# A transformer block on one core: new durations for the order's planner, SyncE issues held back by one planned microsecond, fifteen weight corrections moved from VectorE to ScalarE and GpSimd

## The chip, the core and the metric

The kernel runs on one core of a Trainium2 chip (trn2). The metric is the device time of one execution in microseconds (us), as the median of several runs. One profiled execution lies beside the timed runs; all rows of the profile come from it.

## What is computed

A transformer block over 2048 tokens of width 640: layer norm, sliding-window attention with 32 heads of size 20 and a window of 256 keys, output projection and residual, then layer norm, a GEGLU feed-forward of width 1536, and residual. All inputs and the output are float32.

```python
def _A_ref(x, wqkv, wo):            # B, S, D = 1, 2048, 640
    H = 32; Dh = D // H; W = 256
    qkv = (x @ wqkv).reshape(B, S, 3, H, Dh).transpose(2, 0, 3, 1, 4)
    q, k, v = qkv[0], qkv[1], qkv[2]
    scores = jnp.einsum("bhqd,bhkd->bhqk", q, k) * (Dh ** -0.5)
    mask = (idx[:, None] - idx[None, :] >= 0) & (idx[:, None] - idx[None, :] < W)
    scores = jnp.where(mask[None, None], scores, -1e9)
    p = softmax(scores)
    return einsum("bhqk,bhkd->bhqd", p, v).transpose(0, 2, 1, 3).reshape(B, S, D) @ wo
def _B_ref(x, w_gate, w_up, w_down):
    return (gelu_tanh(x @ w_gate) * (x @ w_up)) @ w_down
h = x + _A_ref(layernorm(x), A_wqkv, A_wo)
out = h + _B_ref(layernorm(h), B_w_gate, B_w_up, B_w_down)
```

## The kernel before

**Numbers.** Float32 factors are split into a high and a low float16 part, and a product is three float16 matmuls (high by high, high by low, low by high). Each weight matrix W is scaled by a power of two `sc` and split by a `Weight` object: its high part `hl[0]` is made by ScalarE (`split`), its low part `hl[1]` = W·sc − high by a task `low`, one per slice of 128 rows. `low` has two forms. Without `spread`, VectorE does it in one `scalar_tensor_tensor`. With `spread`, ScalarE first scales the slice of W in place and GpSimd then subtracts the high part. A matrix is `ready` when all its low slices are made, and only then may the matmuls that read it be ordered.

**Weights.** `load_lane` brings the output projection and the first gate and up matrices (`w3`, and `gu` in the trace) in slices through a ring of three buffers `wsl`, each slice twice: once for the maximum that gives `sc`, once to be split. A ring buffer is free again when `low` is done with it. The later feed-forward matrices come whole through one buffer `wst`, and of each of these two slices already take the `spread` form.

**Stages.** 16 blocks of 128 tokens, in 8 chunks of two for q and k. Normed x blocks (`xh`, `xl`) are turned by DMA transposes; q and k of a chunk are projected (`mm` banks), leave through `qks` to DRAM and come back stacked by head (`qT`, `kT`). For each block and each pair of heads there are two visits to the score banks `ra` and `rb`: a *maxima* unit (scores in one orientation, reduced on VectorE by the operation that the trace calls `CUSTOM_DVE_ANT_0 junk<-ra,band`, one per head), and, once the row maxima have been put into `qT` through `mT`, a *scores* unit (the other orientation, exponentiated by ScalarE into `pt`, cut to the band by GpSimd's affine selects). Four heads then make a *value* unit (`pv`). Then come normalisation, transposes, the output projection with the residual (`ht`), and a store of the block to `h_dram`. The first feed-forward product runs under the end of the attention; after the attention come three plain (chunk, group) products and then nine "quads" groups, whose matmul order is written out.

TensorE works in three modes: full products, row mode (maxima and scores, 64 rows each) and column mode (values, 32 columns each).

**The order.** Nothing in this kernel is ordered by hand before the quads. Each piece of work is a generator ("lane") that yields the engines it needs and the planned time at which its operands are there. At build time a loop advances a planned clock `now` and always steps the first lane in a list of priorities whose `start(now)` holds; the instruction it emits is booked on that engine with a cost from `Engine.cost`. So `cost` sets no time on the chip, only the order of instructions on each engine. On the chip each engine works its own list strictly in order, waiting at semaphores. The planner puts two units of row work (a maxima and a scores unit, as a rule) into one visit to row mode if the second bank is planned to come free within `APART` = 1.0 us (`row_need`). When no score has been made yet and TensorE is planned to be idle, the loop emits a small dummy matmul on `pv`.

A DMA on SyncE's queue is ordered when `need() <= now + 0.1` for its lane: loads of x and of the residual, the stores to `h_dram`, the DMA transposes, the stacking loads of q and k (lane `stack`), weights (`load_lane`).

Of the kernel before, what the change touches and what calls it, by code (L numbers as in the profile page):

```python
# [24 lines left out]
KC = D // P  # L25
# [9 lines left out]
SWITCH = 0.095  # L35
# [18 lines left out]
class Clock:  # L54
# [90 lines left out]
    def warmth(self, cost, rows):  # L145

        k = int(self.t["tensor"] / self.WINDOW)
        if k > self.win:
            u = self.use / self.WINDOW if k == self.win + 1 else 0.0
            self.warm = u > 0.4 if self.warm else u > 0.75  # L150
            self.win, self.use = k, 0.0
        if not self.warm:
            cost *= 2
        self.use += cost * rows / 128
        return cost
# [34 lines left out]
class Engine:  # L190
# [23 lines left out]
    def cost(self, op, out, ins):  # L214
        n = out.free_size()
        if op.startswith("dma_start"):
            size = math.prod(c for _, c in out.ap) * mybir.dt.size(out.dtype)
            if op == "dma_start_transpose":
                return size / 150e3
            wide = mybir.dt.size(out.dtype) == 4 or out.space == DRAM  # L220
            return size / (380e3 if wide else 150e3)
        half = mybir.dt.size(out.dtype) == 2 and ins and mybir.dt.size(ins[0].dtype) == 2
        if self.name == "tensor":
            n = ins[1].free_size()
            if op == "transpose":
                n = ins[0].partition_size()
            passes = 1 if mybir.dt.size(ins[0].dtype) == 2 else 2 if op == "transpose" else 4
            rows, cols = ins[0].partition_size(), out.partition_size()
            mode = "full" if op == "transpose" else "row" if rows <= 64 else "col"
            mode = "full" if mode == "col" and cols > 32 else mode  # L230
            k = self.clock
            switch, k.mode = SWITCH * (k.mode != mode), mode
            at = out.start_partition() + (ins[0].start_partition() // 4 if mode == "row" else 0)
            beside, k.half = mode != "full" and at > k.half and not switch, at
            if beside:
                return 0.004
            return switch + k.warmth(max(n * passes / 2400, 0.027), rows) + 0.0027
        if self.name == "vector":
            m = max([n] + [i.free_size() for i in ins])
            if op == "tensor_copy" and half or op == "tensor_scalar" and m > 320:  # L240
                return (0.065 if half else 0.185) + 0.00053 * m
            return 0.065 + 0.00106 * m + 0.06 * (op == "scalar_tensor_tensor" and len(ins) == 3)
        if self.name == "scalar":
            return 0.00084 * n + (0.05 if op == "copy" or len(ins) == 1 else
                                  0.14 if ins[0].space == PSUM else 0.18)
        if self.name == "gpsimd":
            if op == "memset":
                return 0.06 + 0.0008 * n
            return 0.46 if n == 1 else 0.06 + (0.00105 if op == "affine_select" else 0.00203) * n
        raise NotImplementedError(self.name)  # L250


# [1 line left out]
def block_kernel(ctx: ExitStack, tc: tile.TileContext, x, wqkv, wo, wg, wu, wd, out):  # L254
# [27 lines left out]
    def done(name):  # L282
# [12 lines left out]
    NW, AHEADQ = 3, 6  # L295
    SPREAD = 0
# [5 lines left out]
    FFBACK = dict(split_lane=0.4, scale_lane=0.4, chunk_lane=0.3, token_sums=0.1,  # L302
                  sums_lane=0.2, norm_lane=0.2)
    EARLY = 0.6
    PACE = 1.0
    SWAY = 4

# [12 lines left out]
    def on(eng, *reads, when=None, after=None):  # L320
        f = need(*reads, when=when, eng=eng)
        if after is not None:
            return (eng,), lambda: max(f(), nc.others(after, eng))
        return (eng,), f
# [214 lines left out]
    def products(n, term, ready=None, at_=None):  # L539


        ps = [at_[0]] if at_ else []
        col = at_[1] if at_ else 0

        def start(i):
            if ready and not ready(i) or not ps and opened["mm"] >= banks["mm"]:
                return INF
            t = nc.ready([x for ab in term(i) for x in ab], "tensor")
            return t if ps else max(t, nc.slot(psums["mm"], "mm", banks["mm"]))

        for i in range(n):
            yield ("tensor",), lambda i=i: start(i)
            if not ps:
                ps.append(bank("mm"))
            m = term(i)
            for k, (l, r) in enumerate(m):
                if k:
                    yield pe()
                o = ps[0][:, col:col + r.free_size()]
                nc.tensor.matmul(o, l, r, start=(i == 0 and k == 0),  # L560
                                 stop=(i == n - 1 and k == len(m) - 1))
                pos["dense"] += r.free_size() * 3 // len(m)
        return o
# [19 lines left out]
    wq = wqp.enter_context(tc.tile_pool(name="wq", bufs=1, side="right"))  # L583
    wp = attn.enter_context(tc.tile_pool(name="wp", bufs=1))
# [3 lines left out]
    gu = ffw.tile([P, 4 * KC * 512], F16, name="gu")  # L588
# [3 lines left out]
    gu = gu.rearrange("p (a c f) -> p a c f", c=KC, f=512)  # L592
# [174 lines left out]
    def stack(c, which, d):  # L767
# [10 lines left out]
        for par in range(2):  # L778
            for m, i in enumerate(((0, 0, 1), (0, 1, 0))[which]):
                rows = slice(64 * par + DH * m, 64 * par + DH * m + DH)  # L780
                if c > 1:
                    yield ("sync",), lambda: nc.moved["sync"] - PACE
                nc.sync.dma_start(to[rows], d.rearrange("(a d i) m n -> a m d i n", a=2,
# [652 lines left out]
    def split_lane():  # L1436
        for i, w in [(1, weights[1]), (0, weights[0]), *enumerate(weights)][:2] + list(
                enumerate(weights))[2:]:
            yield on("scalar", when=lambda: w.scaled)
            if i <= NW:  # L1440
                yield from w.split(wq if i < NW else wp, SPREAD)
                continue
            yield on("scalar", when=lambda: W["v"].ready)
            kind, fg = later[i - NW - 1]
            if fg == 0 and kind != "d":
                a = 2 * (kind == "u")
                yield from w.split((gu[:, a], gu[:, a + 1]))
                continue
            k = 1 if fg else 0
            yield on("scalar", when=lambda: ffpools[k])  # L1450
            yield from w.split(ffpools[k], 2)
# [106 lines left out]
    class Lane:  # L1558
# [11 lines left out]
        def start(self, now):  # L1570

            if "tensor" in self.engs:
                return nc.t["tensor"] <= now + AHEAD and self.need() <= max(now, nc.t["tensor"])
            name = self.gen.__name__
            back = self.back
            if name in ("split_lane", "scale_lane"):
                back = PREP if not W["o", 0].ready else FFPREP
            elif name == "x_lane":
                back = EARLY if not B[XF].full else LATE
            elif name == "max_out" and not W["v"].ready:  # L1580
                back = RAMPMAX
            if isinstance(self.engs, Soon):
                back = max(back, OUT)
            if ffpools[1]:
                back = FFBACK.get(name, OUT)
            return (all(nc.t[e] <= now + back for e in self.engs if e != "sync")
                    and self.need() <= now + 0.1)

    load_x(0)
    load_x(1)  # L1590
# [3 lines left out]
    for i, n in enumerate("qkv"):  # L1594
        W[n].load(rooms[n])
        W[n].room(wq)
        if i:
            load_x(i + 1)
    load_x(NR)
    lanes = [x_lane([0], "x"), x_lane([1], "xb"), x_lane([2], "xc"), x_lane([3], "xd"),  # L1600
             x_lane(range(NR, NB), "x"),
             split_lane(), *(scale_lane([i], str(i)) for i in range(NW)),
             scale_lane(range(NW, len(weights)), "0"), load_lane(), ones_lane(), big_lane(),
             first_norm_lane()]
# [6 lines left out]
    now = 0.0  # L1611
# [85 lines left out]
```

## Time and profile before

| | |
|---|---|
| median of 3 runs | 1022.13 us (1021.41 to 1023.31) |
| profiled execution, its own time | 1023.17 us |
| its span, first to last instruction | 1021.3 us |
| TensorE (PE) busy | 999.8 us, 98% |
| VectorE (DVE) busy | 754.8 us, 74% |
| ScalarE (ACT) busy | 437.0 us, 43% |
| GpSimd (POOL) busy | 298.0 us, 29% |
| granted TensorE clock | 1.000 |

Between span and time lie 1.87 us. In the trace every instruction carries line L199, since a helper records all of them, so groups are told apart by their tiles: `w3l<-wsl,sw,w3h` is a low part of the output projection, `gu<-wsl,sw,gu` one of the first gate or up matrix. PEld is the weight load, which overlaps PE. SPq is SyncE's queue of DMA issues. A busy PE is not PE at its peak: matmuls are pipelined, so a matmul's own duration is longer than the distance to the next one.

### The profile page before, as it was taken

What the parts mean: (1) busy time and instruction counts of PE and PEld (TensorE: products, weight loads), DVE (VectorE), ACT (ScalarE), POOL (GpSimd) and SP (SyncE); (2) the same over time, 40 slices, a digit from 0 to 9 for tenths busy, and PEclk for the clock granted to TensorE, in tenths of its full rate; (3) what the DMA queues carried; (4) which work ended last, traced back from release to release, by engine and by line L of the source; (5) the groups of instructions that cost most, each with busy time, mean ns of one, the idle gap of its engine ahead of it and who ended that gap; (6) DMA issues with size and microseconds to landing.
All of it is one profiled execution on the core that took longest, in us unless ns stands there. A gap on an engine that the chain in (4) does not pass through costs nothing.

```text
span 1021.3 us, 30777 instructions
## 1 busy us (share of the span) xinstructions
PE 999.8 (98%) x12921; PEld 695.8 (68%) x12921; DVE 754.8 (74%) x2221; ACT 437.0 (43%) x706; POOL 298.0 (29%) x489
## 2 busy tenths in 40 slices
PE   8999999999999999999999999999999999999998
PEld 7875666676666676776655564567777777777776
DVE  6888998986787787474788788798996975544553
ACT  6514654656555564654558543522222222221220
POOL 7102223443343342342436321255313310000000
PEclk9999999999999999999999999999999999999999
DMA  8657667361551524225033433223553532222211
GB/s 306 137 116 175 184 145 168 81 163 55 91 122 44 114 57 118 42 61 127 3 131 106 92 117 103 78 104 127 161 177 90 161 138 78 78 96 86 78 53 52
DMA packets 105835, 112.67 MB, mean 110 GB/s; under 512 B 38369, under 2 KB 79585, under 8 KB 105697
## 3 DMA queue, kind: packets, MB, share of 16 engines
q1 hardware_dynamic: 93600, 99.97, 35.9%
q10 hardware_dynamic: 12096, 10.75, 3.4%
q8 instruction: 101, 1.65, 0.7%
q14 instruction: 38, 0.30, 0.1%
HBM read 73.73 MB, written 28.84 MB: 100 GB/s over the span
## 4 chain that ended last, share of the span: by engine, by line
PE 82%; DVE 8%; DMA 4%; ACT 2%; issue 2%; SPq 1%; POOL 0%; ACTq 0%; DVEq 0%
PE mm L199 41%; PE pv L199 12%; PE ra L199 11%; PE rb L199 10%; PE tp L199 7%; DVE junk L199 2%; DVE am L199 1%; DVE ht L199 1%; DMA v<-in_wqkv_dram 1%; DMA gu<-in_wqkv_dram 1%; SPq L199 1%; DMA qT<-mT 1%; DVE m L199 1%; ACT pt L199 1%; DMA h_dram<-ht 1%
## 5 line engine op out<-in xcount | busy, mean ns | idle before, releaser
L199 POOL TENSOR_SCALAR_AFFINE_SELECT pt<-pt 128x512 f32<-128x512 f32 x352 | 175.3, 513 | 278.2 <-ACT pt L199 262.6
L199 DVE CUSTOM_DVE_ANT_0 junk<-rb,band 128x320 bf16<-128x320 f32 x230 | 112.5, 489 | 41.3 <-PE rb L199 35.9
L199 DVE CUSTOM_DVE_ANT_0 junk<-ra,band 128x320 bf16<-128x320 f32 x218 | 106.6, 489 | 43.8 <-PE ra L199 38.3
L199 ACT ACTIVATE pt<-ra,esc 128x640 f32<-128x640 f32 (+2 forms) x131 | 99.6, 767 | 66.2 <-PE ra L199 53.3
L199 ACT ACTIVATE pt<-rb,esc 128x640 f32<-128x640 f32 (+2 forms) x125 | 94.9, 766 | 77.2 <-PE rb L199 56.5
L199 PE MATMUL pv<-pt,v 128*21 128x128 f32 x2880 | 104.1, 275 | 1.1 <-ACT oT L199 1.1
L199 PEld LDWEIGHTS <-ah 128*128 128x128 f16 x768 | 75.0, 98 | 29.5 <-issue 2.1
L199 ACT ACTIVATE gel<-gel,ffk 128x512 f32<-128x512 f32 x36 | 26.0, 721 | 138.0 <-DVE gel L199 138.0
L199 PEld LDWEIGHTS pv<-pt,v 128*21 128x21 f32 x2880 | 68.6, 100 | 11.9 <-issue 2.1
L199 PEld LDWEIGHTS <-ws 128*128 128x128 f16 x720 | 70.3, 98 | 8.3
L199 PEld LDWEIGHTS <-kT 62*64 62x64 f16 x2880 | 61.9, 107 | 13.9 <-issue 10.1
L199 PEld LDWEIGHTS <-qT 60*64 60x64 f16 x1280 | 29.8, 104 | 60.3 <-issue 51.3
L199 PEld LDWEIGHTS <-gu 128*128 128x128 f16 x440 | 42.1, 98 | 36.1 <-issue 2.5
L199 DVE SCALAR_TENSOR_TENSOR ht<-mm,ffk,ht 128x320 f32<-128x320 f32 x96 | 52.1, 545 | 10.9 <-PE mm L199 9.0
L199 ACT CAST ah<-gel 128x512 f16<-128x512 f32 x48 | 29.6, 617 | 64.4 <-DVE gel L199 64.2
L199 PE MATMUL mm<-xh,w1h 128*128 128x256 f16 x200 | 54.7, 274 | 1.3 <-DVE qks L199 1.3
L199 PE MATMUL mm<-xl,w1h 128*128 128x256 f16 x200 | 54.7, 273 | 0.0
L199 PE MATMUL mm<-xh,w1l 128*128 128x256 f16 x200 | 54.7, 273 | 0.0
L199 PE MATMUL mm<-w3l,oh 128*128 128x320 f16 x160 | 48.1, 301 | 0.1
L199 PE MATMUL mm<-w2h,xh 128*128 128x320 f16 x160 | 48.1, 300 | 0.0
L199 PE MATMUL mm<-w2h,xl 128*128 128x320 f16 x160 | 48.1, 301 | 0.0
L199 PE MATMUL mm<-w3h,ol 128*128 128x320 f16 x160 | 48.1, 300 | 0.0
(299 smaller groups left out, 2521.3 us busy)
## 6 DMA issues: line engine op xcount, KB each, us to landing
ws<-wsums SPq DMA_DIRECT2D x24, 640.0 KB
qk<-qks ACTq DMA_DIRECT2D x32, 256.0 KB
qT<-qk SPq DMA_DIRECT2D x48, 160.0 KB
kT<-qk SPq DMA_DIRECT2D x48, 160.0 KB
wsums<-ws SPq DMA_DIRECT2D x12, 640.0 KB
ht<-in_x_dram SPq DMA_DIRECT2D x16, 320.0 KB
h_dram<-ht SPq DMA_DIRECT2D x16, 320.0 KB
ht<-h_dram SPq DMA_DIRECT2D x16, 320.0 KB
```

The costliest lines, as they stand in the source:

```text
L199: r = real(*args, **kw)
```

## The change

Three things. The planner's cost function gets other constants. A lane on SyncE alone, other than `stack` and `load_lane`, is ordered only when its operands have been there for `HELD` = 1.0 planned us (before: up to 0.1 us ahead of them). And the low parts of the output projection (5 slices of 128x640) and of the first gate and up matrices (5 slices of 128x512 each) take the `spread` form.

```diff
@@ Engine.cost
-            switch, k.mode = SWITCH * (k.mode != mode), mode
+            switch = (SWITCH + 0.02 * (k.mode == "col")) * (k.mode != mode)
+            k.mode = mode
...
             if beside:
-                return 0.004
+                return 0.0005
...
-            return 0.065 + 0.00106 * m + 0.06 * (op == "scalar_tensor_tensor" and len(ins) == 3)
+            extra = {"reciprocal": 0.16, "tensor_tensor_reduce": 0.11}.get(op, 0.0)
+            extra += 0.06 * (op == "scalar_tensor_tensor" and len(ins) == 3)
+            return 0.065 + 0.00106 * m + extra
         if self.name == "scalar":
-            return 0.00084 * n + (0.05 if op == "copy" or len(ins) == 1 else
+            return 0.03 + 0.00084 * n + (0.05 if op == "copy" or len(ins) == 1 else
                                   0.14 if ins[0].space == PSUM else 0.18)
         if self.name == "gpsimd":
             if op == "memset":
                 return 0.06 + 0.0008 * n
-            return 0.46 if n == 1 else 0.06 + (0.00105 if op == "affine_select" else 0.00203) * n
+            return 0.46 if n == 1 else 0.1 + (0.00105 if op == "affine_select" else 0.00203) * n
@@ block_kernel
+    HELD = 1.0
@@ split_lane
-                yield from w.split(wq if i < NW else wp, SPREAD)
+                yield from w.split(wq if i < NW else wp, SPREAD if i < NW else KC)
...
-                yield from w.split((gu[:, a], gu[:, a + 1]))
+                yield from w.split((gu[:, a], gu[:, a + 1]), KC)
@@ Lane.start
+            late = 0.1 if self.engs != ("sync",) or name in ("stack", "load_lane") else -HELD
             return (all(nc.t[e] <= now + back for e in self.engs if e != "sync")
-                    and self.need() <= now + 0.1)
+                    and self.need() <= now + late)
```

`SPREAD` is 0 and `KC` is 5. `tensor_tensor_reduce` is the maxima operation.

## The prediction

> **What bounds the kernel now.** I read the page first, then the busy time by stretches, then who TensorE waits for in two windows, then single rows of the timeline.
>
> ```profile
> PE 999.8 (98%) x12921; PEld 695.8 (68%) x12921; DVE 754.8 (74%) x2221; ACT 437.0 (43%) x706; POOL 298.0 (29%) x489
> ```
>
> TensorE is the bound over the whole span. Its work is the same after the change: no matmul is added or removed but the dummies. So the time can only move through what stands between matmuls: waits, changes of mode, dummies.
>
> ```profile
> 90.00:200.00 110.00, 104.07 (x1728) 71.20 (x1727) 99.79 (x348) 66.43 (x116) 35.64 (x65) 1.00 0.62 155
> ...
> 677.00:1022.00 345.00, 340.86 (x2543) 248.16 (x2541) 230.26 (x452) 77.84 (x121) 67.09 (x63) 1.00 0.32 104
> ```
>
> The columns are window, length, then busy time of PE, PEld, DVE, ACT, POOL. From 677 on the matmul order is written out and TensorE is busy to within 4 us (345 - 340.86), the end of the program included: I cost the change at nothing there. From 90 to 200, where all fifteen moved low parts lie, VectorE is at 99.79 of 110, close to being a second bound. What TensorE waits for, first from 90 to 200, then from 200 to 677 (total, times, longest, in us):
>
> ```profile
> PE rb L199 <- issue: 1.3, 1, 1.3
> PE rb L199 <- DMA qT<-mT: 1.1, 1, 1.1
> PE rb L199 <- DVE mxs L199: 0.7, 1, 0.7
> PE pv L199 <- ACT oT L199: 0.7, 2, 0.4
> PE rb L199 <- ACT pt L199: 0.6, 1, 0.6
> PE tp L199 <- DVE ht L199: 0.5, 1, 0.5
> PE mm L199 <- DVE qks L199: 0.5, 1, 0.5
> PE ra L199 <- ACT pt L199: 0.2, 1, 0.2
> ```
>
> ```profile
> PE tp L199 <- DVE m L199: 1.4, 4, 0.8
> PE rb L199 <- issue: 1.1, 1, 1.1
> PE mm L199 <- DVE ht L199: 1.1, 2, 0.7
> PE ra L199 <- DMA kT<-qk: 0.8, 1, 0.8
> PE tp L199 <- DVE am L199: 0.7, 1, 0.7
> PE tp L199 <- DVE ol L199: 0.6, 1, 0.6
> PE tp L199 <- ACT oT L199: 0.5, 1, 0.5
> PE tp L199 <- DVE ht L199: 0.4, 1, 0.4
> PE pv L199 <- ACT oT L199: 0.4, 1, 0.4
> PE mm L199 <- ACT gel L199: 0.3, 1, 0.3
> ```
>
> They sum to 5.6 and 7.3 us, 12.9 in all. The two "issue" rows (2.4) name no engine, so no order of the others removes them; 10.5 us are within reach. Of these VectorE causes 5.9 (0.7 + 0.5 + 0.5 + 1.4 + 1.1 + 0.7 + 0.6 + 0.4), ScalarE and DMA 4.6. So the kernel is already near its bound and the change is worth at most about 1% of it.
>
> **The new durations.** Whether they are nearer to the chip can be read off the timeline, by distances from start to start:
>
> ```profile
> 239.73 0.33 PE L199 MATMUL ra<-kT,qT 60*64 60x256 f16 x8
> 239.89 0.31 PE L199 MATMUL rb<-qT,kT 62*64 62x128 f16 x12
> 240.13 0.85 PE L199 MATMUL pv<-pt,v 128*21 128x128 f32 x24
> 240.92 0.28 PE L199 MATMUL mm<-xh,w1l 128*128 128x256 f16 x1
> 241.04 0.27 PE L199 MATMUL mm<-xh,w1h 128*128 128x256 f16 x1
> 241.15 0.27 PE L199 MATMUL mm<-xl,w1h 128*128 128x256 f16 x1
> 241.35 0.33 PE L199 MATMUL rb<-kT,qT 60*64 60x256 f16 x8
> ```
>
> ```profile
> 226.00 0.49 DVE L199 CUSTOM_DVE_ANT_0 junk<-ra,band 128x320 bf16<-128x320 f32 x1 [0.67 <-PE ra L199]
> 226.42 0.08 DVE L199 DVE_READ_ACCUMULATOR2_ANT mxs<- 128x1 f32 x1
> 226.54 0.49 DVE L199 CUSTOM_DVE_ANT_0 junk<-ra,band 128x320 bf16<-128x320 f32 x1
> ```
>
> TensorE took 0.16 for a maxima unit, 0.24 for a scores unit with the change to column mode, 0.79 for a value unit with the change back: 1.19 us. By the code the old costs book 0.163 + 0.273 + 0.779 = 1.215, the new ones 0.145 + 0.241 + 0.768 = 1.154. The old were 2% long, the new are 3% short: no gain in itself. VectorE took 0.54 per maxima operation; the old cost is 0.065 + 0.00106 x 320 = 0.404, the new 0.514. This is the correction that matters: the old order was laid out for a VectorE a quarter faster at its most frequent operation, beside a TensorE slightly slower than the real one, so on the chip VectorE falls behind the plan and TensorE meets its results late. With the new costs both are a few per cent short, and their ratio is about right. I take half of VectorE's 5.9 us as gone, 3.0 us. The waits on ScalarE and DMA (4.6) are dealt anew, with the same sum: ScalarE's and GpSimd's constants move by only 0.03 and 0.04 per instruction. Bounds: all 10.5 gone; or as much again added, +10, since a new order makes new coincidences.
>
> **The low parts.** Prices: what leaves VectorE, what comes to GpSimd and to ScalarE (least, median and longest ns; the last three from the later weights, which take that form already):
>
> ```profile
> L199 DVE SCALAR_TENSOR_TENSOR w3l<-wsl,sw,w3h x5: 876/879/1293, 98.9 to 107.8; 128x640 f16<-128x640 f32 x5
> ```
>
> ```profile
> L199 DVE SCALAR_TENSOR_TENSOR gu<-wsl,sw,gu x10: 731/746/1026, 144.2 to 197.1; 128x512 f16<-128x512 f32 x10
> ```
>
> ```profile
> L199 POOL TENSOR_TENSOR w10l<-wst,w10h x2: 1396/1396/1397, 540.2 to 542.4; 128x640 f16<-128x640 f32 x2
> ```
>
> ```profile
> L199 POOL TENSOR_TENSOR w5l<-wst,w5h x2: 1156/1158/1159, 588.5 to 589.9; 128x512 f16<-128x512 f32 x2
> ```
>
> ```profile
> L199 ACT ACTIVATE wst<-wst,sw x14: 721/722/830, 539.3 to 679.1; 128x512 f32<-128x512 f32 x8, 128x640 f32<-128x640 f32 x6
> ```
>
> VectorE loses 5 x 0.879 + 10 x 0.746 = 11.9 us of its 99.79. ScalarE gains 5 x 0.83 + 10 x 0.72 = 11.4 on its 66.43, GpSimd 5 x 1.396 + 10 x 1.158 = 18.6 on its 35.64: 71% and 49% of 110, so neither becomes a bound. What VectorE's relief is worth at TensorE is bounded by the three waits on it in that window, 1.7 us, half of which is counted above; I take another 0.8. Each part is now finished about 0.83 + 1.40 later than its high part instead of 0.88, so a ring buffer comes free some 1.3 us later and the output projection's weights are ready perhaps 3 us later; its first matmul has projections of q, k and v to stand in for it, so 0, and 3 if these run out.
>
> Against this stands one row:
>
> ```profile
> 542.46 1.40 DVE L199 TENSOR_SCALAR m<-mxs 128x32 f16<-128x32 f32 x1
> ```
>
> A VectorE instruction on 32 columns took 1.40 us while GpSimd's `w10l` subtraction of 1.396 us (second of its two, 542.4) ran, and it is the longest of TensorE's waits on `m` above, 0.8 us. So such a subtraction can hold a short VectorE instruction to its own end. [...] From the rows: fifteen subtractions cover 18.6 of 110 us, 17%; some four blocks put out two such `m` instructions each there, so one or two are hit, at 0.8 us: I take +0.8. Bounds: 0, and 15 x 0.8 = +12 if each hits.
>
> **The held issues.** SyncE works in order, and most of its waiting is on the store's data:
>
> ```profile
> SPq L199 <- DVE ht L199: 219.1, 29, 40.8
> ```
>
> Behind a store stand the next loads, turns and stacking loads; ordering the store 1 us later lets what is planned in that microsecond go ahead. But TensorE's list names a stacked load only once (0.8) and no load or turn of x at all, so little is waiting behind. In return the first feed-forward norm, which overwrites `ht`, waits for the store:
>
> ```profile
> 233.50 0.61 DVE L199 TENSOR_SCALAR ht<-ht,lmvh,lyh 128x640 f32<-128x640 f32 x1 [1.72 <-DMA h_dram<-ht]
> ```
>
> Four blocks do this, and TensorE's waits on `ht` at `tp` (0.5 and 0.4) are what reaches it. I take 0; bounds -0.8 and +4 x 1.0. Turns and loads of x, ordered 1 us later each, cost nothing while the next chunk is a block ahead.
>
> **The sum.** -3.0 - 0.8 + 0.8 + 0 = -3.0 us. The profiled execution took 1023.17 (span 1021.3 and 1.87 around it), which gives 1020.2; the median of the runs shown lies 1.04 lower, so 1022.13 - 3.0 = 1019.1 us, 0.3% faster. A difference of about 0.2% (2 us) is what a measurement of this kernel can tell from none.
>
> **The rivals.**
>
> *Single visits (slower).* The plan pairs two units in a visit if the second bank comes free within 1.0 us. Booking 0.11 more for each of the two operations of a maxima unit frees its bank 0.22 later in the plan. A visit with one unit pays the entry once more (241.15 to 241.35 is 0.20, where such a product followed by another takes 0.11) and, at the planner's 0.095, the way out: 0.19 us. Against: visits lie 1.62 apart (239.73, 241.35), a bank needs 2 x 0.514 and some 0.2 of latency, 1.2, so the pairs hold with 0.4 to spare. They break where VectorE has something else in hand, which is 90 to 200. It decides if over 25 pairs break: 25 x 0.19 = 4.8, against the gain of 3.0, is 1024; 40 make 1027.
>
> *GpSimd in the way (slower).* Instead of one hit, eight to twelve, at `m` and in front of the affine selects that the value units wait for: +6 to +10 in place of 0.8, so 1024 to 1028; it decides from six hits.
>
> *Dealt anew, nothing won (same).* The waits named on VectorE vanish and others of the same size come: 1022.
>
> *All waits gone (faster still).* 10.5 us: 1011.6. Against: DMA and ScalarE waits have no better duration in the new plan.
>
> **How the numbers follow.** Forecast (gain of 2.1 to 7, 1015 to 1020): 0.42. Larger gain: 0.10. Same: 0.17. Single visits: 0.18. GpSimd in the way: 0.13. So faster 0.52, same 0.17, slower 0.31. The likeliest case's own range is 1015 to 1020; to leave out no more than 2 in 10 the range goes from 1011 (all waits gone) to 1027 (40 broken pairs).
>
> **What would show it.** Right: TensorE's waits on VectorE between 90 and 677 fall from 5.9 to about 3; VectorE's busy time from 90 to 200 falls by some 10; the stretch from the first quads group to the end keeps its length. Wrong: more matmul groups on `ra` and `rb` entered singly; `m` instructions of 1.2 to 1.4 us beside `w3l` or `gu` on GpSimd with TensorE waiting behind them; a first maxima or first score that comes later than now, which I have left at no change.

## The result and the profile after

| | before | after |
|---|---|---|
| median, same chip | 1021.77 us (1020.80 to 1023.31, 4 runs) | 1045.72 us (1044.12 to 1046.28, 4 runs) |
| profiled execution, its own time (span) | 1023.17 us (1021.3) | 1046.20 us (1044.5) |
| mean granted TensorE clock | 1.000 | 0.988 |

The ratio is 1.0233 [1.0215, 1.0251]: 2.3% slower, where 0.3% faster was forecast, and the time lies outside the range of 1011 to 1027. The profile's page after, busy times and the granted clock in 40 slices:

```profile
PE 1020.9 (98%) x13189; PEld 720.1 (69%) x13189; DVE 755.0 (72%) x2206; ACT 449.3 (43%) x721; POOL 315.7 (30%) x504
...
PEclk9999899999999999998899999999999999999999
```

TensorE is still the bound, and now it has 268 matmuls more (13189 against 12921) and slices in which its granted clock is below the full one. No other engine became a bound: VectorE's busy time is what it was. The groups of the dummy matmuls (least, median and longest ns, first and last start), before and after:

```profile
L199 PE MATMUL pv<-ident x324: 218/219/312, 2.5 to 74.3; 128*128 128x128 f16 x162
```

```profile
L199 PE MATMUL pv<-ident x592: 219/219/314, 2.5 to 108.8; 128*128 128x128 f16 x198
```

All 268 are dummies, and they go on 34.5 us longer (74.3 to 108.8). They are ordered while no score has been made, so the first score comes late. The timeline of TensorE after, at that place:

```profile
99.76 0.33 PE L199 MATMUL rb<-kT,qT 60*64 60x320 f16 x4
100.02 3.69 PE L199 MATMUL pv<-ident 128*128 128x128 f16 x63
103.64 0.24 PE L199 MATMUL tp<-ident,m 128*64 128x128 f16 x1
...
104.66 4.36 PE L199 MATMUL pv<-ident 128*128 128x128 f16 x75
108.95 0.24 PE L199 MATMUL ra<-qT,kT 62*64 62x128 f16 x1
111.12 0.30 PE L199 MATMUL ra<-qT,kT 62*64 62x128 f16 x7 [1.93 <-DMA qT<-mT]
```

The first score (`ra<-qT,kT`) comes at 108.95, after ten stretches of dummies from 90.55 on, between which stand only seven maxima units and two transposes of `m`. The last 75 dummies fill 4.29 us (104.66 to 108.95), 0.057 each, so 268 are 15.3 us. The score waits for the row maxima `m`, and these come late in VectorE's order: 80 maxima operations stand ahead of the first of them, 64 before (counted over both traces). The group of the first `m` instruction of each block, before and after:

```profile
L199 DVE TENSOR_SCALAR m<-mxs x16: 130/316/1398, 81.2 to 542.5; 128x32 f16<-128x32 f32 x16
```

```profile
L199 DVE TENSOR_SCALAR m<-mxs x16: 170/178/455, 101.1 to 576.3; 128x32 f16<-128x32 f32 x16
```

The first `m` is at 101.1 instead of 81.2. The second loss is the clock. Stretches of after, with the columns of the prediction's windows and the granted clock behind the five busy times:

```profile
112.20:119.00 6.80, 6.40 (x66) 3.56 (x69) 4.25 (x17) 4.70 (x10) 2.63 (x5) 0.50 0.51 106
...
125.90:129.30 3.40, 3.40 (x33) 2.03 (x32) 2.36 (x7) 3.31 (x7) 1.81 (x2) 0.50 0.76 122
484.30:491.10 6.80, 5.91 (x105) 4.21 (x105) 4.19 (x17) 3.32 (x5) 2.84 (x6) 0.50 0.49 94
515.00:521.80 6.80, 6.02 (x84) 4.24 (x83) 4.45 (x18) 3.70 (x5) 2.85 (x6) 0.50 0.94 329
```

TensorE works 21.7 us at half clock (6.40 + 3.40 + 5.91 + 6.02). If nothing there takes more than twice as long, my estimate from products of 128x256 (0.11 from start to start at 125.55, 0.21 at 128.01, where the clock is 0.50), that costs half of it at most, 10.9; in the profiled execution of before there was none ahead of the last microsecond. The other three timed runs of after had mean clocks of 0.991 to 0.995 and took 1044.12 to 1046.28 us, so this part varies from run to run and the time hardly does. Who TensorE waits for after, from 90 to 200 and then from 200 to 677:

```profile
PE rb L199 <- DVE mxs L199: 2.9, 1, 2.9
PE ra L199 <- DMA qT<-mT: 1.9, 1, 1.9
PE ra L199 <- ACT pt L199: 0.8, 1, 0.8
PE rb L199 <- ACT pt L199: 0.2, 1, 0.2
```

```profile
PE rb L199 <- ACT pt L199: 2.4, 3, 0.9
PE ra L199 <- ACT pt L199: 1.7, 3, 0.9
PE pv L199 <- POOL pt L199: 0.7, 3, 0.3
```

With the three rows of 0.2 to 0.3 that are not shown they are 11.4 us against 12.9 before. But the work ahead of the quads, which ended at 670.9 before, goes on to 693.0 after, and behind 677 TensorE has two more waits there, the second in the first quads group:

```profile
PE mm L199 <- DVE ht L199: 1.4, 1, 1.4
PE tp L199 <- DVE ws L199: 1.9, 1, 1.9
```

Over the whole trace its waits are 19.2 us, 17.3 before. So 15.3 of dummies, at most 10.9 of half clock and 1.9 of waits come to at most 28.1, against 23.0 measured between the two profiled executions. The 5.1 between are not resolved. Two parts of them can be seen: at half clock not every distance doubles (from a maxima to a scores unit it is 0.14 at 480.53 and 0.22 at 485.66, in rows shown further below), and TensorE changes its mode nineteen times fewer (counted over both traces; in the prediction's rows a visit starts 0.20 after a product, and a next product 0.11 after it). The waits are nearly as long as before, and yet the kernel is 2.3% slower: most of what it lost is time spent on dummies and at half clock, and neither is a wait.

### The profile page after: what moved, and what is told of

The parts are those of the page before. It is cut to its first block, busy times and chain, and to the rows that moved or that the text cites. A ratio compares the mean times of both kernels' runs of the same rounds, so it can differ in the third digit from the quotient of the medians.

```text
span 1044.5 us, 31321 instructions
## 1 busy us (share of the span) xinstructions
PE 1020.9 (98%) x13189; PEld 720.1 (69%) x13189; DVE 755.0 (72%) x2206; ACT 449.3 (43%) x721; POOL 315.7 (30%) x504
## 3 DMA queue, kind: packets, MB, share of 16 engines
q1 hardware_dynamic: 93600, 99.97, 34.5%
## 4 chain that ended last, share of the span: by engine, by line
PE 87%; DVE 6%; DMA 3%; ACT 2%; issue 1%; SPq 1%; POOL 0%; ACTq 0%; POOLq 0%; DVEq 0%
PE mm L199 43%; PE pv L199 14%; PE ra L199 12%; PE rb L199 10%; PE tp L199 7%; DVE ts L199 1%; SPq L199 1%; ACT pt L199 1%; DMA qk<-qks 1%; DMA kT<-qk 1%; DMA qT<-mT 1%; DMA wst<-in_wu_dram 0%; DVE ht L199 0%; DVE am L199 0%; DVE junk L199 0%
## 5 line engine op out<-in xcount | busy, mean ns | idle before, releaser
L199 DVE CUSTOM_DVE_ANT_0 junk<-ra,band 128x320 bf16<-128x320 f32 x226 | 110.7, 490 | 57.2 <-PE ra L199 52.2
L199 DVE CUSTOM_DVE_ANT_0 junk<-rb,band 128x320 bf16<-128x320 f32 x222 | 108.8, 490 | 52.9 <-PE rb L199 48.3
L199 ACT ACTIVATE pt<-rb,esc 128x640 f32<-128x640 f32 (+2 forms) x128 | 98.9, 777 | 84.1 <-PE rb L199 73.1
L199 ACT ACTIVATE pt<-ra,esc 128x640 f32<-128x640 f32 (+2 forms) x128 | 95.8, 757 | 86.1 <-PE ra L199 80.7
L199 PE MATMUL pv<-pt,v 128*21 128x128 f32 x2880 | 107.1, 279 | 0.8 <-POOL pt L199 0.7
L199 PEld LDWEIGHTS <-kT 62*64 62x64 f16 x2880 | 65.6, 108 | 14.2 <-issue 10.4
L199 DVE SCALAR_TENSOR_TENSOR ht<-mm,ffk,ht 128x320 f32<-128x320 f32 x96 | 52.0, 544 | 15.3 <-PE mm L199 13.4
L199 POOL TENSOR_TENSOR gelt<-gelt 128x256 f32<-128x256 f32 x18 | 15.4, 854 | 112.1 <-ACT gelt L199 112.0
L199 PE MATMUL mm<-xl,w0h 128*128 128x256 f16 x175 | 48.9, 280 | 0.0
L199 PE MATMUL mm<-xh,w0h 128*128 128x256 f16 x175 | 48.9, 279 | 0.0
L199 PE MATMUL mm<-xh,w0l 128*128 128x256 f16 x175 | 48.9, 279 | 0.0
```

Source lines behind the costliest of these rows:

```text
L199: r = real(*args, **kw)
```

## The experiments

With each set of kernels, before was run on the same chip (medians 1021.8 to 1022.9). A ratio is to that before.

**Which part of the change does it.** First the change without the 0.11 of the maxima operation, and that 0.11 alone in the kernel before:

```diff
e1: the changed kernel, with
-            extra = {"reciprocal": 0.16, "tensor_tensor_reduce": 0.11}.get(op, 0.0)
+            extra = {"reciprocal": 0.16}.get(op, 0.0)
e2: the kernel before, with
+            extra = {"tensor_tensor_reduce": 0.11}.get(op, 0.0)
```

> The changed kernel without one number: the 0.11 that the planner's cost adds to each maxima operation. Held issues, GpSimd's low parts and all other new costs stay. Theory A (that one cost): in the program as written 64 maxima operations stand before the first row-maximum instruction m, as in the kernel before, instead of 80, and 335 dummies instead of 592; so the first score comes at about 90 us as before, the clock stays at 1.000 and the time is 1014 to 1024. Theory B (the low parts crowd ScalarE and GpSimd, or delay the output projection) and theory C (the held issues delay SyncE): both are still in, so 1040 to 1046.

> The kernel before with one number changed: the 0.11 on each maxima operation. Theory A: 80 maxima operations before the first m and 578 dummies, first score at about 109 us, time 1036 to 1048. Theories B and C: neither low parts nor held issues are in, so as before, 1020 to 1024.

Measured: e1 1026.30, ratio 1.0037 [1.0019, 1.0054]; e2 1044.02, ratio 1.0199 [1.0161, 1.0236]. One number in the planner's table makes some 20 of the 24 us, and theories B and C are out as the main cause. In e2 the dummies are 578, in e1 335. e1 lies 2 us above theory A's range, which is part of the 4 us taken up below.

Then the parts that are no durations: the old table with the held issues and the low parts, and each of these alone.

```diff
e3: the changed kernel with the cost function of before
e7: the kernel before, with
+            late = 0.1 if self.engs != ("sync",) or name in ("stack", "load_lane") else -HELD
e8: the kernel before, with
+                yield from w.split(wq if i < NW else wp, SPREAD if i < NW else KC)
+                yield from w.split((gu[:, a], gu[:, a + 1]), KC)
```

> The changed kernel with all the old costs: held issues and GpSimd's low parts alone. Theory A: 64 maxima operations before the first m, 324 dummies, time 1016 to 1025, and which side of before it falls tells what the two other parts are worth. Theories B and C: 1040 to 1046.

> The kernel before with the held issues alone. Held issues and low parts together, with the old costs, took 1025.8 against 1022.64. If the held stores are the cause (the first feed-forward norm waits for them: the wait of 2.3 us on ht at 150 us there): 1024 to 1028 here and 1021 to 1023 with the low parts alone. If it is neither by itself but where the transition to the feed-forward falls: both within 1020 to 1026 with no pattern.

> The kernel before with the fifteen low parts on ScalarE and GpSimd alone. Held stores as the cause of the 3 us: 1021 to 1023. Low parts as the cause (the output projection's first product comes at 130 us instead of 115, short VectorE instructions held by GpSimd): 1024 to 1028. My prediction had this part at 0 net.

Measured: e3 1025.80, ratio 1.0029 [1.0011, 1.0046]; e7 1023.16, ratio 1.0010 [0.9995, 1.0026]; e8 1026.58, ratio 1.0040 [1.0023, 1.0057]. The held issues alone cost nothing clear, the low parts alone 4 us.

**Why a longer, seemingly truer booking does harm.** `junk`, the unused output of the maxima operation, has one buffer. The planner's clock already charges for that:

```python
                lat = self.LAT if e != eng else (0.1 if e in ("vector", "gpsimd") else 0.0)
...
        if len(ring) == bufs:
            self.wr[key] = [((0, 128, 0, 1 << 30), "ring", self.quiet(ring[0]))]
```

A tile whose ring of buffers is full counts as written by "ring", which is no engine, so its next writer waits `LAT` = 0.18 after the last use.

Two maxima operations in a row were thus booked 0.404 + 0.18 = 0.584 apart, not 0.404, and the change makes that 0.694. The chip takes 0.534 (median over both traces). Booked at what the chip takes, with one buffer:

```diff
e9: the changed kernel, with
-            extra = {"reciprocal": 0.16, "tensor_tensor_reduce": 0.11}.get(op, 0.0)
+            extra = {"reciprocal": 0.16, "tensor_tensor_reduce": -0.05}.get(op, 0.0)
```

> The whole changed kernel, one junk buffer, with -0.05 instead of +0.11 on the maxima operation, so that with the 0.18 for the buffer the planner books 0.534, the distance that the trace shows for it (0.534 in the median). The two runs with a second junk buffer were not a test of the plan alone: there the chip's distance fell too, from 0.534 to 0.416. A2 (a VectorE booked too slow spoils the order): about as the run without the 0.11, which booked 0.584: 1018 to 1028. If the 0.11's harm had to do with something else that the second buffer happens to mend on the chip: 1034 or more.

Measured: 1027.05, ratio 1.0044 [1.0024, 1.0063]: the 20 us are gone, as in e1. With a second buffer the plan adds no 0.18, and the 0.11 should be harmless:

```diff
e5: the changed kernel, e6: e2 and e11: the kernel before, each with
-            junk = at("junk", [P, 5 * HB], BF16, 1)
+            junk = at("junk", [P, 5 * HB], BF16, 2)
```

> The whole changed kernel, 0.11 included, with two buffers instead of one for junk, the maxima operation's unused output. The run with m put first took back the late first score and no time, so theory A is now this (A2): with one buffer the planner books 0.18 more between two maxima operations, as a wait for the buffer, so before the change it booked 0.404 + 0.18 = 0.584 for what takes 0.54 on the chip, and with the change 0.694: counted twice. A VectorE booked a quarter too slow holds row visits back, projections are used up ahead of the scores, and TensorE has no cover later. With two buffers that wait is gone and the booking is 0.514: by A2 the time falls to 1015 to 1028, the half-clock windows in the attention go, the share of projections done at 400 us falls from 0.83 to 0.78 to 0.80. Rival D: the 0.11 harms by what it does to the order in any case, or the other new costs do: 1036 to 1046.

> The kernel before with the 0.11 and with two buffers for junk, nothing else. A2: the one number that cost 21 us by itself costs nothing once it is not counted twice: 1016 to 1027. Rival D: 1036 to 1046.

> The kernel before with two junk buffers, its old costs, nothing else: booked 0.404, done in 0.416 by the chip. A2: a booking that fits and 0.118 us less for VectorE at each of 512 operations (55 us of its time): 1012 to 1020, faster than before and than the run with 0.11. If VectorE's time is hidden anyway: 1018 to 1024.

Measured: e5 1026.61, ratio 1.0044 [1.0027, 1.0061]; e6 1019.74, ratio 0.9988 [0.9969, 1.0007]; e11 1022.85, ratio 1.0007 [0.9988, 1.0026]. The 0.11 that costs 21 us with one buffer costs nothing with two. But the chip changes too, in the timeline of VectorE in e6:

```profile
299.53 0.49 DVE L199 CUSTOM_DVE_ANT_0 junk<-rb,band 128x320 bf16<-128x320 f32 x1 [0.80 <-PE rb L199]
299.94 0.08 DVE L199 DVE_READ_ACCUMULATOR2_ANT mxs<- 128x1 f32 x1
299.94 0.49 DVE L199 CUSTOM_DVE_ANT_0 junk<-rb,band 128x320 bf16<-128x320 f32 x1
```

The next operation starts 0.41 after the first, not 0.54 as in the prediction's rows: the second buffer takes out 0.12 on the chip (medians 0.416 and 0.534). So e5 and e6 alone don't tell whether the order or the faster VectorE mended it. Two more do. e11 has the faster VectorE and the old booking, and gains nothing, where I had given 1012 to 1020 for a booking that fits the chip: VectorE's time is hidden, as far as one order shows it (e11's order isn't that of before: its first score comes at 74.6). And e10 has the faster VectorE and is booked 0.694:

```diff
e10: the kernel before, with two buffers for junk and
+            extra = {"tensor_tensor_reduce": 0.29}.get(op, 0.0)
```

> The kernel before with two junk buffers and with 0.29 on the maxima operation: the planner books 0.694 per operation, as in the changed kernel, while the chip does it in 0.416. A2: the order alone does the harm, so 1036 to 1060, with 80 maxima operations before the first m, some 600 dummies and half-clock windows, although VectorE is faster than in any kernel with one buffer. If the chip's VectorE time were the cause: at or below the 1019.7 of the run with 0.11 and two buffers.

Measured: 1072.67, ratio 1.0497 [1.0464, 1.0531]. The maxima operation is as fast as in e11 (0.416 in the median), only the order differs, and it costs 50 us, more than I had expected. Two of its windows at half clock, and its longest waits from 200 to 700, on ScalarE:

```profile
465.50:472.30 6.80, 5.83 (x116) 3.47 (x112) 2.55 (x13) 3.37 (x5) 2.55 (x6) 0.50 0.01 2
496.20:506.40 10.20, 9.07 (x152) 5.96 (x152) 4.63 (x20) 4.67 (x7) 4.25 (x9) 0.50 0.37 72
```

```profile
PE ra L199 <- ACT pt L199: 5.3, 8, 0.9
PE rb L199 <- ACT pt L199: 4.1, 6, 0.9
```

It is the picture of after, larger. (It isn't the plan of e2 on a faster chip: the 0.29 books VectorE as busy, where a ring's 0.18 is only a wait, so this plan is harsher.)

**How the order loses it.** With the maxima booked 30% long, the plan holds row visits apart until it expects a bank to be free. Visits in the prediction's rows lie 1.62 apart with three products between (239.73, 241.35). After, at the same place, in TensorE's timeline:

```profile
239.47 0.33 PE L199 MATMUL rb<-kT,qT 60*64 60x320 f16 x4
...
241.74 0.33 PE L199 MATMUL ra<-kT,qT 60*64 60x320 f16 x4
...
243.67 0.33 PE L199 MATMUL ra<-kT,qT 60*64 60x320 f16 x4
```

They are 2.27 and 1.93 apart, with nine and thirteen products between. From 200 to 530, 43 of before's 177 visits have three matmuls of the full mode (products or transposes) ahead of them and one has fewer than two; after, no visit has three or four, 149 of 163 have five or more, and twelve have one or none (counted over both traces). The products are used up early: at 400 us 82% of the projections but only 55% of the scores are made, before 79% and 62%. The other kernels agree: in e2, e4 and e10 the scores made at 400 us are 56, 56 and 53%, in every other kernel of the experiments 60 to 62% (counted over their traces). What comes then, in the timeline of after:

```profile
480.53 0.34 PE L199 MATMUL ra<-kT,qT 60*64 60x128 f16 x8
480.67 0.34 PE L199 MATMUL rb<-qT,kT 62*64 62x128 f16 x12
480.94 0.24 PE L199 MATMUL tp<-ident,m 128*64 128x128 f16 x1
481.90 0.33 PE L199 MATMUL rb<-kT,qT 60*64 60x128 f16 x8 [0.72 <-ACT pt L199]
482.04 0.34 PE L199 MATMUL ra<-qT,kT 62*64 62x128 f16 x12
482.31 0.87 PE L199 MATMUL pv<-pt,v 128*21 128x128 f32 x16
483.46 0.42 PE L199 MATMUL pv<-pt,v 128*21 128x128 f32 x8 [0.29 <-POOL pt L199]
483.81 0.34 PE L199 MATMUL rb<-kT,qT 60*64 60x128 f16 x8
484.28 0.48 PE L199 MATMUL ra<-qT,kT 62*64 62x128 f16 x12
485.66 0.48 PE L199 MATMUL ra<-kT,qT 60*64 60x128 f16 x8 [0.89 <-ACT pt L199]
485.88 0.53 PE L199 MATMUL rb<-qT,kT 62*64 62x128 f16 x12
```

No `mm` stands between the visits, so the exponentials `pt` are waited for, and from 484.28 the same operation takes 0.48 instead of 0.34: half clock, 0.50 from 484.30 on by the row further above.

One more kernel tried the other end, the late first `m`, by putting the lane of the row maxima ahead of the other maxima lanes:

```diff
e4: the changed kernel, with
+        mfirst = [l for l in trans if l.gen.__name__ == "max_rows"]
-        order = (first + early + outs + trans + sides
+        order = (first + mfirst + early + outs + trans + sides
```

> The whole changed kernel, with one more line in the planner: the lane that turns a block's row maxima into m stands ahead of the maxima operations of later blocks (33 maxima operations before the first m instead of 80, 319 dummies instead of 592). Theory A, with the late m as the link: the first score comes before 90 us and most of the 24 us lost come back: 1020 to 1030 if the later half-clock windows (484 to 491 and 515 to 522 us, worth some 7 us) stay, 1012 to 1020 if they go too. If the cost harms in another way than through the late m, or by theories B and C: 1038 or more.

Measured: 1045.94, ratio 1.0219 [1.0184, 1.0255]. The dummies' group and its waits:

```profile
L199 PE MATMUL pv<-ident x319: 219/219/311, 2.5 to 74.0; 128*128 128x128 f16 x160
```

```profile
PE ra L199 <- ACT pt L199: 5.6, 8, 1.1
PE tp L199 <- DVE ws L199: 4.4, 1, 4.4
```

All 268 extra dummies are gone, the first score is at 80.0, and the time is the same: the lost time moves to waits on `pt` and `ws` and to 23.8 us at half clock (five windows, at 0.50 or 0.51). So the late first score, the link that I had given theory A, is not what costs, and the dummies aren't the cause. As I read it, they are one form in which a plan with too little for TensorE to do shows.

**What is left: about 4 us.** The low parts alone cost 4 us (e8), where I had 0. Split:

```diff
e13: the kernel before, with
+                yield from w.split(wq if i < NW else wp, SPREAD if i < NW else KC)
e14: the kernel before, with
+                yield from w.split((gu[:, a], gu[:, a + 1]), KC)
```

> The kernel before, with the low parts of the output projection's five weights alone made by GpSimd. All fifteen low parts by GpSimd, with nothing else changed, had cost 4 us (1026.58), and the first product of the output projection had come at 132.5 instead of 115. Theory L1 (the output projection's weights come ready later, and its products are then missing as cover): nearly all of the cost is here, 1025 to 1028. Theory L2 (each low part on GpSimd holds VectorE or is itself late, so that the cost goes by their number): a third of it, 1023 to 1024. Theory L3 (every other order deals TensorE a few other waits): anything from 1020 to 1029, and the waits that make it up are at places that have nothing to do with these weights.

> The kernel before, with the low parts of the first ten gate and up weights alone made by GpSimd. L1: within 1 us of before, 1021 to 1023. L2: two thirds of the 4 us, 1024 to 1026. L3: anything from 1020 to 1029, by waits that lie elsewhere.

Measured: e13 1018.58, ratio 0.9957 [0.9939, 0.9976], faster, though the output projection's first product comes at 136.1 instead of 115.2; e14 1029.37, ratio 1.0061 [1.0040, 1.0082]. L1 is refuted, and L2 with it (a gain for five parts, a loss for ten). L3's range of 1020 to 1029 misses both as well, by 1.4 and 0.4 us. In e14 one place of loss can be seen, first the wait and then a window:

```profile
PE mm L199 <- ACT ah L199: 2.9, 1, 2.9
```

```profile
595.60:602.40 6.80, 5.72 (x21) 3.00 (x22) 4.88 (x13) 0.39 (x1) 0.00 (x0) 0.50 1.08 209
```

The first down product waits for its activation at 596, some 400 us after the last moved low part (197.1 in the prediction's row), and the half clock behind it costs another 2.9 at most by the same estimate as in after (half of 5.72). The same wait stands in e8 (2.9), and also in e7 (3.1) and e11 (2.7), which move no low part and are not slower than before. So this wait doesn't account for the 4 us by itself, and it lies far from what was edited. That much is left of L3: which waits an order meets. Why five parts gain and ten lose isn't shown.

Then the other new durations, without the 0.11's double count:

```diff
e12: the kernel before, with all new costs but the 0.11, and two buffers for junk
e16: the changed kernel with two buffers for junk and without the low parts by GpSimd
```

> As the run before it (two junk buffers, maxima booked 0.404), with the change's other new costs for TensorE, ScalarE, GpSimd and the reciprocal; no held issues, no low parts. If those costs are worth something: 1 to 5 us below the run with old costs. If they only deal the waits anew: within 4 us of it either way.

> The changed kernel with the second buffer for the maxima's unused output, and without the low parts by GpSimd: all new costs and the held stores stay. The same with the low parts gave 1026.61. If the low parts' 4 us add up whatever the order: 1022 to 1023. If the other new costs (TensorE's switches and waits, the reciprocals, ScalarE's and GpSimd's) are what costs there, as the 1031.42 of all new costs but the 0.11 suggest: 1026 to 1031. L3: anything between.

Measured: e12 1031.42, ratio 1.0077 [1.0050, 1.0104]; e16 1024.37, ratio 1.0021 [0.9997, 1.0045]. e12 lost 8.6 us against e11, more than the 4 either way that I had allowed; in e16 the same costs, with the 0.11 and the held issues, lose nothing clear. So these costs have no price of their own either.

**A version that beats both, and what it is worth.** The best of e6 with the held issues, then the same without its 0.11, and with the low parts that had won in e13:

```diff
e15: the kernel before, with two buffers for junk, the maxima's 0.11 and the held issues
e17: e15 without the 0.11
e18: e15 with the low parts of the output projection by GpSimd
```

> The kernel before, with the maxima's 0.11 added to the booked cost, a second buffer for their unused output (so that the plan adds no wait between two of them), and SyncE's held stores; no low parts by GpSimd and none of the other new costs. Without the held stores this had the lowest median so far (1019.74, ratio 0.9988). If the held stores do nothing, as they did alone (1023.16, ratio 1.001): 1019.5 to 1021. If they help once VectorE is booked as it runs: under 1019. L3: 1018 to 1025.

> The kernel before, with the second buffer for the maxima's unused output and SyncE's held stores, but the old booked cost of 0.404 (the chip takes 0.416 with two buffers). It differs from the run of 1015.16 us by the 0.11 alone. If booking the maxima operation some 0.1 longer than the chip needs it is what helps there (VectorE's results are then early): 1020 to 1024, as without the held stores (1022.85). If the held stores with the second buffer do it: 1014 to 1017.

> The run of 1015.16 us (second buffer, the 0.11, held stores) with the low parts of the output projection by GpSimd as well, which by themselves had a ratio of 0.9957. If that gain belongs to the low parts: 1010 to 1012. If it was the waits dealt anew in that one order: 1014 to 1022.

Measured: e15 1015.16, ratio 0.9919 [0.9894, 0.9944]; e17 1032.94, ratio 1.0103 [1.0075, 1.0131]; e18 1027.83, ratio 1.0054 [1.0028, 1.0080]. e15 is faster than both kernels by more than the runs scatter. But e17 and e18 came out beyond any reading that I had given, and what won 4 us in e13 loses 13 in e18. So e15 is the best of the orders tried and not a rule that was found. Two places where e17 lost can be read off TensorE, the first also off VectorE:

```profile
75.48 0.30 PE L199 MATMUL mm<-w2l,xh 128*128 128x320 f16 x1
80.66 0.79 PE L199 MATMUL tp<-ident,am 128*128 128x128 f32 x2 [4.88 <-DVE am L199]
...
103.45 1.04 PE L199 MATMUL tp<-ident,oT 117*128 117x117 f32 x4 [4.78 <-ACT oT L199]
```

```profile
77.81 0.82 DVE L199 TENSOR_REDUCE am<-wsl 128x1 f32<-128x640 f32 x1 [3.68 <-DMA wsl<-in_wo_dram]
```

The plan put the transpose of a weight's maximum where it expected the weight; the slice landed late, and TensorE stood for 4.88 us. The wait of 4.78 at 103.45 is another kind, on ScalarE's copy `oT`. By what the maxima operation is booked (two in a row, the ring's wait included) minus what the chip takes, all kernels:

| booked minus measured | medians in us |
|---|---|
| -0.01 | 1022.9 (e11), 1031.4 (e12), 1032.9 (e17) |
| 0.00 | 1027.1 (e9) |
| +0.05 | 1022 (before), 1018.6 (e13), 1023.2 (e7), 1025.8 (e3), 1026.3 (e1), 1026.6 (e8), 1029.4 (e14) |
| +0.10 | 1015.2 (e15), 1019.7 (e6), 1024.4 (e16), 1026.6 (e5), 1027.8 (e18) |
| +0.16 | 1044.0 (e2), 1045.7 (after), 1045.9 (e4) |
| +0.28 | 1072.7 (e10) |

Up to +0.10 there is no trend, and the orders lie between 1015 and 1033 whatever was edited; from +0.16 on every kernel loses 20 us or more. The two rows nearest to the chip (-0.01 and 0.00) hold no kernel that is faster than before, so a truer booking was worth nothing by itself.

The booking alone divides the kernels as well: all that book 0.404 to 0.584 lie at 1015 to 1033, all that book 0.694 at 1044 or more. No run books 0.694 for an operation that takes so long, so it stays open whether the difference from the chip does the harm or the length in the plan, beside the planned TensorE. The order is made from the booking alone, and e11's faster VectorE changed nothing, which speaks for the latter.

## Why the prediction was wrong, step by step

**The new durations (-3.0): the step that failed.** I set the cost row alone (0.404 before, 0.514 after) against the chip's 0.54 from start to start. The planner's distance from start to start was 0.584 before and 0.694 after, since it books the one buffer's wait itself, and I had read the cost function and not the clock that calls it. With these numbers the old booking was 9% long and the new 30%, and the sentence that the old order was laid out for too fast a VectorE is the wrong way round. In place of the -3.0 the step cost some +20 us (e2 against before; e10 shows that it is the order), and no bound of mine held that: +10 was the most I allowed for a new order. Even with the distances set right the gain would have been an error: e9, booked at the chip's 0.534, is not faster than before (ratio 1.0044).

What I named as the sign that the step was right came only by the window that I had chosen: TensorE's waits on VectorE between 90 and 677 fell from 5.9 to 3.7 (2.9, and three of 0.2 to 0.3). Counted to the first quads group, 670.9 before and 693.0 after, they are 5.2 and 5.1. Either way the sign told nothing of the time, since this order puts dummies, and products that are missed later, where TensorE would have waited. The other sign, a first score later than before, "which I have left at no change", did come: 90.0 to 108.95. It is the better one, though e4 shows that an early first score doesn't bring the time back.

**The rivals.** *Single visits* began from the right place, VectorE booked later in the plan, but priced the wrong consequence. Its own working, 2 x 0.514 and 0.2 of latency against visits 1.62 apart, left 0.4 to spare; with 2 x 0.694 it is 1.59 of 1.62, and next to nothing is spare. The visits weren't broken into single ones (259 in all, 264 before, counted over the trace) but moved apart. *GpSimd in the way* didn't come: the longest such `m` instruction after is 0.455, against 1.398 before (0.648 against 0.399 for the second kind), so not even the one or two hits of 0.8 in the sum are there, and TensorE's waits on GpSimd's `pt` are 0.7 in all.

**The low parts (0, bounds 0 to +12).** The two groups that left VectorE had taken 12.6 us there by their means (5 x 0.961 and 10 x 0.783), of which 11.9 was forecast; GpSimd's median was 1.407 for `w3l` and 1.158 for `gu`, against 1.396 and 1.158 taken. So each price was right. That VectorE's busy time from 90 to 200 fell from 99.79 to 87.19 doesn't show it: after, that stretch holds less work of the attention (299 instructions of VectorE, 348 before), and in e8, where only the low parts moved, it fell to 97.52. The delay of the output projection was mis-sized: its first product comes 17 us later in e8 (132.5 against 115.0) and 21 in e13, where I had perhaps 3 for its weights. That this costs nothing held in e13, which is not slower. What came of the low parts was +4 (e8), and of their two halves -4 and +6 (e13, e14).

**The held issues (0).** Right alone (e7, ratio 1.0010 [0.9995, 1.0026]). Beside the second buffer it came to -5 with the 0.11 (e15 against e6) and +10 without (e17 against e11), so this too is the order and no price of its own.

**The quads (0).** Right, to 1.1 us. The stretch from the first quads group to the end, before and after:

```profile
670.90:1022.00 351.10, 346.27 (x2584) 252.08 (x2581) 236.29 (x467) 78.79 (x122) 69.21 (x65) 1.00 0.31 102
...
693.00:1045.00 352.00, 346.22 (x2584) 252.49 (x2581) 240.73 (x466) 78.87 (x122) 72.97 (x68) 1.00 0.33 107
```

The spans end at 1021.3 and 1044.5, so 4.1 us are not busy before and 5.3 after; the wait of 1.9 on `ws` shown above is in the latter. My 677 lay 6 us behind the start of the quads.

**The range.** It reached 1027, on the ground that a new order makes at most as much new waiting as there is waiting (10.5). The runs of the corrected bookings spread over 18 us with no trend, so a range for any edit of this planner's inputs has to be some 10 us to each side before the edit's own sign is looked at.

**Open** is what makes one of those orders better than another by up to 18 us, beyond the single waits shown; whether the 0.11's harm sets in at a point or grows along the way, and by which of the two measures; and 5.1 us of the account of the two profiled executions.

## What to carry to other kernels

Before a planner's cost is corrected against the trace, add up everything that the planner books between two starts (cost, latency, waits for buffers), and compare that with start to start; a cost alone is not its duration. Don't count a truer booking as a gain until a run shows it. In an order made by a greedy planner, sum small edits only for what they add to the bound engine: their waits are dealt anew, and two that win apart can lose together (e13 and e15, then e18). When a kernel is slower and its waits are hardly longer, look for filler work and for the granted clock.

## What the hardware showed that I had not expected

**The clock halved without a long wait.** Where the granted clock fell, it read 0.50 (0.51 once, in e4), in stretches of 3.4, 6.8 or 10.2 us: 6.8, 3.4, 6.8 and 6.8 in after, 10.2 in e10. In the 3.41 us ahead of the four of after, TensorE was busy for 0.77, 1.63, 2.23 and 2.25. Ahead of the first and the third, with its busy time behind the length:

```profile
108.83:112.24 3.41, 0.77 (x20) 0.47 (x18) 0.00 (x0) 0.78 (x3) 0.00 (x0) 1.00 1.10 296
...
480.89:484.30 3.41, 2.23 (x68) 1.17 (x58) 2.11 (x9) 1.73 (x3) 1.42 (x3) 1.00 0.32 101
```

The first holds a wait of 1.93, the other no wait above 0.72, only row and column work with little between. What brings half clock on is not shown.

**One output buffer cost 0.12 per operation.** Two maxima operations of 128x320 on VectorE start 0.534 apart when they write the same unused buffer (before and after) and 0.416 apart with two (0.41 in the rows of e6), and VectorE's busy time is 754.8 in before and 732.1 in e6. None of it shows in e11's time (1022.85 against 1022.87), with TensorE as the bound (busy for 98% in before and in e6).

**Runs of one kernel differed with its clock.** e13 took 1016.07 us at a mean granted clock of 1.000 and 1022.59 at 0.995; the profiled run was the latter. A difference of a few us between two kernels has to be read with the clock of their runs beside it.
